# Attention and a gated MLP on one core: one up product split a second time, the softmaxes re-timed, a scheduler that looks ahead

## The chip, the cores and the metric

The kernel runs on one core of a Trainium2 chip, in one launch. The metric is the device time in microseconds, lower is better: the median of several runs, and for all reasoning one execution that was recorded by the hardware profiler.

## What is computed

The input x has 2048 rows of 1024 numbers in bf16. With xn, the layer norm of x, the result is x + s * g. s is an attention over a sliding, dilated window, projected back; g is the silu of a gated MLP on the same xn. Cut to what matters:

```
qkv = xn @ wqkv                      # 32 heads of 32
idx = pos[:, None] - 2 * arange(8)   # each row sees 8 rows: itself, 2 back, 4 back, ... 14 back
logits = einsum("bhsd,bhswd->bhsw", q, k[idx]) * 32 ** -0.5     (masked where idx < 0)
s = einsum("bhsw,bhswd->bhsd", softmax(logits), v[idx]) @ wo
h = silu(xn @ w1) * (xn @ w3)        # 3584 wide
g = silu(h @ w2)
out = x + s * g
```

## The kernel before, in words

**Blocks and chunks.** The rows are worked in two blocks of 1024 (`b` = 0, 1), each of two chunks of 512; the chunks are numbered 0 to 3. Everything is kept turned, features on the 128 partitions, tokens along the free axis. Within a block the order on TensorE is: q, k, v projections (`qkv_pairs`), in block 1 then the output projection of chunk 1 (`wo`), 14 up steps (`up_step`, each for 256 of the 3584 columns of w1 and w3), the down projection (`mlp_down`), the output projection of the block's first chunk, and at the very end that of chunk 3.

**Seven products instead of eight.** Each large product is done by a Strassen scheme: the operand pair is cut 2 x 2, and seven products of sums of the quarters take the place of eight. The two output columns blocks of an up step are gate (w1) and up (w3), the rows are the two chunks. Sums of weight quarters (`w_sums`, line 359 of the helper `tt`) are made by DVE in block 0, used there, stored to DRAM by POOL (`s_dram`) and loaded again in block 1; sums of xn quarters (`xn_sums`) lie in `xs`. In the down projection two of the products (`product2_p1`, `product2_t1`) are split a second time in the same way; their matmuls have 256 columns and line 1102, all others have line 350 (helper `mm`) and mostly 512 columns.

**An up step** has three pairs of PSUM banks, `pa`, `pe`, `pb`. On TensorE: first product into `pa` (8 matmuls), second into `pe` (8), the tail of the step before (8, into its `pb`), fourth into `pa` (8), then 8 each into `pb`, `pe` and `pb` again; the step's own tail is left for the next step. 56 matmuls in all. ACT copies the first product from `pa` into `pb` (`fork`), saves `pe` and `pb` to SBUF in between (`us5`, `us2`) and does the silus; DVE adds `ua2` (from `pe`), `uh` (from `pb`, before the tail writes there again) and multiplies `um`.

**Attention** is DVE's work. `scores(c)`: for each of 8 window positions two multiplications of 2048 elements, three additions, the last of them into `E`. `softmax(c)`: the scores are moved by 16 DMAs, alternately on POOL and SP, so that each partition has whole rows of them; DVE adds up the four parts (three additions `z` of 1024), subtracts the maximum, ACT takes the exponential (with a table load), DVE makes the sum, the reciprocal and the product, and 16 DMAs move the result back, into `E` or, for chunk 2, into a buffer of its own. `values(c)`: 16 multiplications and 14 additions of 2048 elements into `qo`. Softmax and values of a chunk lie beside the matmuls of some later stage.

**Parks.** vT and kT hold one chunk. Chunk 1's k and v, chunk 2's v and chunk 3's q, k and v are staged in h_sb, written to DRAM (`put`) and loaded when their place is free (`get`).

**What sets the order.** The kernel first lists operations with an engine, what they read and write, and an estimated duration (`Plan.op`); `place` gives buffers, `depend` finds the dependences, `limits` works back from TensorE's order to a latest start for each operation, `soon` shifts some of them. `simulate` then runs engines against each other with the estimated durations: TensorE keeps its listed order, any other engine that is free takes, of the operations that are ready, the one with the earliest limit. The resulting order is emitted and fixed: each engine works its instructions in that order, and an instruction that waits holds up everything behind it on that engine. Loads go over SP, most stores over POOL and SP, in six 1 MB buffers (`r8`).

Of the kernel before, what the change touches and what calls it, by code (L numbers as in the profile page):

```python
# [34 lines left out]
class Op:  # L35
    __slots__ = ("eng", "emit", "rd", "wr", "occ", "lat", "table", "nbytes", "pred", "succ", "n",
                 "start", "done", "ready", "limit", "name", "late", "idx", "rate", "then")


class Plan:  # L40
# [3 lines left out]
    def __init__(self):  # L44
        self.ops, self.slots, self.pools, self.wide = [], [], {}, {}
        self.shift = 0.0
        self.rate = 3e5
        self.rank, self.soon, self.chains = {}, {}, []

# [11 lines left out]
    def op(self, eng, name, emit, rd=(), wr=(), occ=0.0, lat=0.08, table=None, nbytes=0, late=0.0):  # L61
        o = Op()
        o.then = None
# [67 lines left out]
    def limits(self):  # L131
# [6 lines left out]
        for o in reversed(self.ops):  # L138
# [6 lines left out]
            o.limit = lim if o.limit is None else min(o.limit, lim)  # L145
            o.limit += o.late
# [9 lines left out]
    def simulate(self):  # L156
# [6 lines left out]
        pipe = 0.0  # L163
# [11 lines left out]
        while left:  # L175
# [13 lines left out]
            if e == PE:  # L189
                o = ops[pes[pe_at]]  # L190
                pe_at += 1
            else:
                i = min((i for i in ready[e] if ops[i].ready <= T), key=lambda i: (ops[i].limit, i))
                ready[e].remove(i)
                o = ops[i]
# [35 lines left out]
def kernel(  # L231
# [12 lines left out]
    P = 128  # L244
# [17 lines left out]
    CH_ = [r.split() for r in ("ofork0_1 exp1", "dfork1_3 exp3", "u2_l10_1 sq2", "fk_l10_1 var2_1")]  # L262
# [15 lines left out]
    s_dram = dram.tile([FB, P, 4, KH, 2 * P], FP16, name="s_dram")  # L278
    t_dram = dram.tile([P, FH, 4, CH], FP16, name="t_dram")
    park = {k: dram.tile([P, NJ, CH], BF16, name=f"park_{k[0]}{k[1]}")  # L280
            for k in (("k", 1), ("v", 1), ("v", 2), ("q", 3), ("k", 3), ("v", 3))}
# [26 lines left out]
    for n, t in plan.wide.items():  # L308
# [13 lines left out]
    nc.gpsimd.memset(maskb[:], 0.0)  # L322
    nc.gpsimd.affine_select(
        out=maskb[0:32], in_=maskb[0:32], compare_op=ALU.is_ge, fill=-1.0e9,
        base=0, pattern=[[-DIL, W], [1, HALO]], channel_multiplier=0,
    )
    nc.gpsimd.memset(kT[:, :, 0:HALO], 0.0)
# [248 lines left out]
    def halo(nm):  # L576
        b = {"k": kT, "v": vT}[nm]
        plan.op(ACT, f"halo{nm}", lambda: nc.scalar.copy(out=b[:, :, 0:HALO], in_=b[:, :, CH:CH + HALO]),
                [(nm, j) for j in range(NJ)], [(nm, j, "halo") for j in range(NJ)], 0.25, 0.11)

    def home(c, nm):

        if (nm, c) in park:
            return lambda j: (lambda: stage(c, nm, j), stage_cells(c, nm, j))
        if nm == "q":
# [4 lines left out]
    def stage_at(c, nm, j):  # L590
        if nm == "q":
            return 20 + j, 1
# [10 lines left out]
    def put(c, nm):  # L603
        cells = [x for j in range(NJ) for x in stage_cells(c, nm, j)]
        fl, _ = stage_at(c, nm, 0)
        if nm == "q":
            src = lambda: h_sb[:, fl:fl + NJ, CH:BL]
        else:
            src = lambda: h_sb[:, fl:fl + 4, :].rearrange("p f (r n) -> p (f r) n", r=2)
        dma(SP, f"put{nm}{c}", lambda: park[nm, c][:], src, cells, [("park", nm, c)], 1024)  # L610

    def get(c, nm, behind=()):
        rd = [("park", nm, c)]
        if c >= 2:
            rd.append(("step", 1, {("v", 2): 2, ("q", 3): 3, ("k", 3): 4, ("v", 3): 5}[nm, c]))
# [38 lines left out]
    def qkv_sums(wts, early=0.0, hold=([], [], [])):  # L654

        S = [plan.slot("r8", f"S{i}") for i in range(2)]
        w = lambda kh, r: (lambda: wts[kh].ap().rearrange("p (c j) -> p c j", j=NJ)[:, :, r * 4:r * 4 + 4])
# [5 lines left out]
        tt("qs2" + "f" * (early > 0), sub, sv(2), w(0, 0), w(0, 1), [wts[0]] + hold[2], c(2), 2048, True, -early)  # L663
        return S
# [71 lines left out]
    def scores(c):  # L736
# [3 lines left out]
        if ("k", c) in park:  # L740
            halo("k")
            get(c, "k", [("E", W - 1, 3, NR - 1)] if c == 1 else [("L", 2)])
        for w in range(W):
            o = HALO - DIL * w
            pr = []
            for jh in range(2):
                p_t = plan.slot("att", f"p{c}_{w}_{jh}")
                tt(f"qk{c}", mul, lambda p_t=p_t: r4(p_t), lambda jh=jh: qo[:, u, jh * 4:jh * 4 + 4, :],
                   lambda jh=jh, o=o: kT[:, jh * 4:jh * 4 + 4, o:o + CH],
                   qo_cells(u, J4[jh]) + [("k", j) for j in J4[jh]] + ([("k", j, "halo") for j in J4[jh]] if w else []),  # L750
# [8 lines left out]
               [p0], [("E", w, sq, r) for sq in range(4) for r in range(NR)], 512, True)  # L759

    def softmax(c):

        zf = lambda a: (lambda: a().bitcast(FP32))
        if c != 2:
            sl = [plan.slot("att", f"sm{c}_{i}") for i in range(3)]
# [856 lines left out]
```

## Time and profile before

| | us |
|---|---|
| median of 3 runs (lowest, highest) | 712.68 (712.26, 712.99) |
| the profiled execution | 712.41 |
| its span, first to last instruction | 710.6 |
| stretch from 30 to 130 us: DVE busy | 99.9 of 100 |
| up steps of block 1, 340 to 600 us: DVE busy | 247.0 of 260 |
| granted TensorE clock | 1.00 throughout |

The profiled execution's time is its span and 1.8 us around it. "Busy" is the time in which an engine had an instruction running. In the timeline a row has its start, its length, the engine, the line of the kernel (often that of a helper), the output and inputs by their buffers' names, the shape, and the number of instructions merged in it; behind it, in brackets, the idle time before it and what ended that. A matmul's row lasts longer than its share of the stream, since matmuls overlap; the distance between starts is what counts.

### The profile page before, as it was taken

How to read it: one execution, taken by the hardware profiler on the slowest of the kernel's cores; microseconds unless marked ns; L12 is line 12 of the kernel's file. 1: busy time of each engine (PE TensorE's matmuls, PEld its weight loads, DVE VectorE, ACT ScalarE, POOL GpSimd, SP SyncE). 2: the span in 40 equal slices, each digit the busy share in tenths (PEclk: the TensorE clock that was granted, in tenths of full speed). 3: DMA queues.
4: the chain of work that ended last, by engine and by line, in shares of the span. 5: the costliest groups of instructions: out<-in, count | busy, mean ns of one | idle time of the engine just before them, and what ended most of it. 6: DMA issues, size and time to landing. Idle time of an engine off the chain costs nothing.

```text
span 710.6 us, 9461 instructions
## 1 busy us (share of the span) xinstructions
PE 704.8 (99%) x3510; PEld 359.2 (51%) x3510; DVE 670.4 (94%) x806; ACT 385.8 (54%) x674; POOL 47.0 (7%) x96
## 2 busy tenths in 40 slices
PE   8999999999999999999999999999999999999998
PEld 5555544444444474744555554444444445656443
DVE  8999999797999999997899999968999997999996
ACT  7644556575656799422535355658565655422233
POOL 1010100202000000002200000020200011020000
PEclk9999999999999999999999999999999999999999
DMA  9999976659545757793654559786653557648503
GB/s 333 289 367 321 322 277 208 207 203 265 200 144 192 257 185 185 178 302 122 221 173 145 178 199 314 260 267 192 174 192 119 183 180 231 208 137 293 178 1 118
DMA packets 131197, 151.35 MB, mean 213 GB/s; under 512 B 17104, under 2 KB 109136, under 8 KB 125904
## 3 DMA queue, kind: packets, MB, share of 16 engines
q1 hardware_dynamic: 121392, 123.03, 54.7%
q0 software_dynamic: 5104, 26.22, 10.0%
q10 hardware_dynamic: 4656, 1.51, 1.0%
q8 instruction: 27, 0.44, 0.3%
q14 instruction: 18, 0.15, 0.1%
HBM read 106.96 MB, written 32.51 MB: 196 GB/s over the span
## 4 chain that ended last, share of the span: by engine, by line
PE 96%; ACT 2%; DVE 1%; DMA 1%; issue 0%; SPq 0%; DVEq 0%; ACTq 0%
PE mm L350 90%; PE mm L1102 6%; ACT r L474 1%; ACT k L364 1%; DMA r<-in_A_x_dram 1%; ACT k L479 0%; PE mm L529 0%; DVE small L447 0%; ACT L806 0%; DVE r L463 0%; DVE xT L359 0%; ACT a L806 0%; ACT h_sb L381 0%; PE mm L375 0%; SPq L387 0%
## 5 line engine op out<-in xcount | busy, mean ns | idle before, releaser
L350 PEld LDWEIGHTS <-r 128*128 128x128 f16 (+1 forms) x2276 | 240.2, 107 | 244.0 <-DMA r<-in_A_wqkv_dram 0.4
L350 PE MATMUL mm<-xs,r 128*128 128x512 f16 x1280 | 295.3, 379 | 0.0
L350 PE MATMUL mm<-xT,r 128*128 128x512 bf16 (+1 forms) x996 | 227.2, 372 | 0.1
L364 ACT COPY k<-mm 128x512 f32<-128x512 f32 (+1 forms) x200 | 115.1, 579 | 75.3 <-PE mm L350 68.4
L350 PE MATMUL mm<-r,h_sb 128*128 128x512 f16 (+1 forms) x592 | 129.6, 379 | 0.0
L350 PEld LDWEIGHTS <-h_sb 128*128 128x128 f16 (+1 forms) x688 | 67.3, 98 | 80.3 <-issue 0.6
L364 ACT COPY mm<-mm 128x512 f32<-128x512 f32 (+1 forms) x105 | 56.4, 541 | 59.6 <-PE mm L350 41.0
L359 DVE TENSOR_TENSOR a<-a,a 128x2048 bf16<-128x2048 bf16 (+1 forms) x68 | 82.6, 1215 | 0.1
L359 DVE TENSOR_TENSOR a<-qo,kT 128x2048 bf16<-128x2048 bf16 x64 | 77.0, 1215 | 0.1
L381 ACT ACTIVATE k<-k 128x512 bf16<-128x512 f32 x56 | 33.0, 625 | 68.3 <-DVE k L359 68.2
L359 DVE TENSOR_TENSOR r<-r,r 128x1024 f16<-128x1024 bf16 (+6 forms) x71 | 60.0, 851 | 0.7 <-DMA xT<-r 0.5
L359 DVE TENSOR_TENSOR h_sb<-mm,k 128x512 bf16<-128x512 f32 (+1 forms) x68 | 59.2, 900 | 0.7 <-PE mm L350 0.7
L359 DVE TENSOR_TENSOR h_sb<-h_sb 128x1024 f16<-128x1024 bf16 (+7 forms) x55 | 43.9, 822 | 7.1 <-DMA h_sb<-E 3.6
L359 DVE TENSOR_TENSOR a<-E,vT 128x2048 bf16<-128x2048 bf16 x42 | 49.7, 1215 | 0.0
L359 DVE TENSOR_TENSOR k<-mm,k 128x1024 f32<-128x1024 f32 (+1 forms) x44 | 44.8, 1022 | 3.7 <-PE mm L350 3.7
L381 ACT ACTIVATE h_sb<-mm 128x512 bf16<-128x512 f32 x60 | 35.8, 599 | 17.6 <-PE mm L350 16.9
L364 ACT CAST k<-mm 128x512 bf16<-128x512 f32 x56 | 32.6, 587 | 13.5 <-PE mm L350 13.5
L359 DVE TENSOR_TENSOR h_sb<-h_sb,k 128x2048 bf16<-128x2048 bf16 x28 | 34.1, 1217 | 6.1 <-ACT k L364 6.1
L359 DVE TENSOR_TENSOR qo<-qo,a 128x2048 bf16<-128x2048 bf16 x32 | 38.9, 1214 | 0.0
L359 DVE TENSOR_TENSOR a<-a 128x1024 bf16<-128x1024 bf16 (+4 forms) x53 | 33.7, 638 | 2.4 <-ACT a L806 2.2
L359 DVE TENSOR_TENSOR r<-r 128x1024 f16<-128x1024 bf16 (+3 forms) x37 | 28.7, 801 | 0.0
L387 POOL DMA_DIRECT2D a<-E x24 | 12.5, 527 | 174.1 <-DVE E L359 95.3
(120 smaller groups left out, 480.6 us busy)
## 6 DMA issues: line engine op xcount, KB each, us to landing
r<-in_B_w_dram SPq DMA_DIRECT2D x42, 512.0 KB, 5.0
s_dram<-r POOLq DMA_DIRECT2D x14, 1024.0 KB, 5.4
r<-t_dram SPq DMA_DIRECT2D x16, 896.0 KB, 7.1
r<-s_dram SPq DMA_DIRECT2D x14, 1024.0 KB, 5.0
r<-in_B_w_dram SPq DMA_DIRECT2D x12, 896.0 KB, 5.5
r<-in_A_wqkv_dram SPq DMA_DIRECT2D x10, 1024.0 KB, 7.2
h_sb<-in_B_w_dram SPq DMA_DIRECT2D x14, 512.0 KB, 9.1
t_dram<-h_sb POOLq DMA_DIRECT2D x7, 1024.0 KB, 5.5
```

The source lines that it names most:

```text
L350: nc.tensor.matmul(cut(ps.ap()), lhsT=lhs[k](), rhs=cut(rhs[k]()), start=(first and k == 0), stop=(last and k == n - 1), skip_group_check= ...
L359: plan.op(DVE, name, lambda: fn(out=o(), in0=a(), in1=b()), rd, wr, occ, 0.08, late=late)
L364: plan.op(ACT, name, lambda: nc.scalar.copy(out=o(), in_=a()), rd, wr, occ, 0.11)
L381: plan.op(ACT, name, lambda: nc.scalar.activation(out=o(), in_=a(), func=ACTF.Silu), rd, wr, occ, 0.11, table="silu")
L387: plan.op(eng, name, lambda: e.dma_start(out=o(), in_=a()), rd, wr, occ, 0.0, nbytes=kb * 1024, late=late)
L474: plan.op(ACT, f"mean{c}_{st}", lambda i=i, st=st: nc.scalar.activation(out=xrow(xt, st), in_=xrow(xt, st), func=ACTF.Copy, scale=1.0 / D, ...
L1102: nc.tensor.matmul(half(bank.ap, n)(), lhsT=a[k](), rhs=c[k](), start=first and k == 0, stop=k == NQ - 1, skip_group_check=True)
```

## The change

1. **A second split in the up stage.** In block 1, from step 1 on, the first product (into `pa`) is made of seven products of half-size matmuls, two each, in four parts that are put between the products of the step before (`up_first`). It needs sums of w1's quarters (`w_sums2`, made by DVE in block 0 for steps 1 to 13, stored by POOL, loaded on SP with 256 KB a step) and of the first chunk's xn (`x_sums2`, four sums, once). Between the parts stand three ACT copies of 256 columns and one DVE addition (`ucc`) of 512.
2. **Moves in halves.** As soon as four of the eight window positions are there, their scores are moved (`gather`), in four DMAs of twice the size in place of eight; the additions `z` and the product behind the reciprocal are made in halves as well, and each half of the result is moved back by itself.
3. **Places.** Softmax 2 and 3 work in h_sb (rows of it that late up steps fill). k3 isn't parked but written to h_sb, where the scores read it; v2 stays staged in h_sb and is copied to vT by one DMA.
4. **Softmax 3** is listed behind the scores of chunk 3, in the up stage ahead of values 2; before it stood behind the output projection of chunk 2.
5. **The scheduler** simulates three times ahead of the real one and notes when each operation became ready. An ACT or DVE operation is now held back, and the engine left idle, if it would run past the time at which a more urgent one is to become ready and would make that one late.
6. The masks for the first rows are made in a scratch buffer and spread by a small DMA at the start.

```diff
+            o.need = o.limit
             o.limit += o.late
...
+                for i in sorted((i for i in ready[e] if ops[i].ready <= T), key=lambda i: (ops[i].limit, i)):
+                    o = ops[i]
+                    end = T + o.occ + (1.29 if o.table and o.table != table else 0.0)
...
+                            if q.start is None and q is not o and q.limit < o.limit:
+                                hurt = end - max(q.need + lag, q.eta)
+                                if hurt > 0.05 + self.look[e] * (q.eta - T):
+                                    hit = q
+                                    break
...
+        for _ in range(self.passes):
+            self.simulate()
+            for o in self.ops:
+                o.eta = o.ready
...
-            for k in (("k", 1), ("v", 1), ("v", 2), ("q", 3), ("k", 3), ("v", 3))}
+            for k in (("k", 1), ("v", 1), ("q", 3), ("v", 3))}
...
-            get(c, "k", [("E", W - 1, 3, NR - 1)] if c == 1 else [("L", 2)])
+            get(c, "k", [("E", W - 1, 3, NR - 1)])
+        if c == 3:
+            halo("k", c)
...
+            if w % 4 == 3:
+                gather(c, w // 4)
...
+    def gather(c, i):
+        sm_places(c, i)
+        L, Lc = SM[c][i][0:2]
+        for r in range(NR):
+            dma((POOL, SP)[r % 2], f"L{c}", lambda r=r: L()[:, r * 512:(r + 1) * 512],
+                lambda r=r: E[r:P:NR, :, 4 * i:4 * i + 4].rearrange("p q w n -> p q (w n)"),
...
-        tt(f"z{c}", add, zv, lambda: Lv(0)[:, 0], lambda: Lv(0)[:, 1], LC[0] + LC[1], zc, 1024, False)
...
+        for i in range(2):
...
+            tt(f"z{c}", add, zi, part(0), part(1), Lc[i](0) + Lc[i](1), zc[i], 512, False)
+            tt(f"z{c}", add, zi, zi, part(2), Lc[i](2) + zc[i], zc[i], 512, False)
+            tt(f"z{c}", add, zi, zi, part(3), Lc[i](3) + zc[i], zc[i], 512, False)
...
+            if b in U2B and fb:
+                dma(SP, f"s2.{fb}", lambda: s2_v(wt).rearrange("p q k n -> p (q k n)"),
+                    lambda: s2_dram[fb].rearrange("p q k n -> p (q k n)"), [("sd2", fb)], [(wt, 1, 0)], 256)
...
+        tt("wss0", add, S(0), A(1, 0), A(1, 1), Ac, Sc(0), 256, True)
+        tt("wss2", sub, S(2), A(0, 0), A(1, 0), Ac, Sc(2), 256, True)
+        tt("wss1", sub, S(1), S(0), A(0, 0), Ac + Sc(0), Sc(1), 256, True)
+        tt("wss3", sub, S(3), A(0, 1), S(1), Ac + Sc(1), Sc(3), 256, True)
...
+    def up_first(b, fb):
...
+            plan.op(PE, "mu " + pa[i].name, emit, A[1] + B[1], [pa[i]], 2 * 0.1097, 0.0)
+
+        p(1, 0, a(0, 0), x(0, 0), True)
+        p(1, 1, s_(0), t(0))
+        s5 = plan.slot("k2", "us5p")
+        cp(f"ufork{b}_{fb}", half(pa[0].ap, 0), half(pa[1].ap, 0), [pa[1]], [pa[0]], 0.27)
+        cp("us5p", half(lambda: f32(s5), 0), half(pa[1].ap, 1), [pa[1]], [s5], 0.27)
+        yield
+        p(1, 0, s_(1), t(1))
+        p(0, 0, a(0, 1), x(1, 0))
+        cp(f"usnap{b}_{fb}", half(pa[0].ap, 1), half(pa[1].ap, 0), [pa[1]], [pa[0]], 0.27)
+        yield
+        p(1, 0, s_(2), t(2))
+        p(0, 1, s_(3), x(1, 1))
...
+        both = lambda: pa[0].both().rearrange("p b n -> p (b n)")
+        tt(f"ucc{b}", add, lambda: both().rearrange("p (b h n) -> p b h n", b=2, h=2)[:, :, 1],
+           lambda: both()[:, HC:3 * HC].rearrange("p (b n) -> p b n", b=2),
+           lambda: f32(s5)[:, 0:HC].unsqueeze(1).to_broadcast([P, 2, HC]), [pa[0], pa[1], s5], [pa[0], pa[1]], 512, False)
+        yield
+        p(1, 0, a(1, 1), t(3))
...
     def up_step(b, fb):
-        for i in I:
+        for i in I if not two else ():
             mm(pa[i], wl(0, 0, i), bx[0, 0], True, [(wt, 0, 0)] + xt_cells(0, 0), mark=[("step", b, fb)])
...
             mm(pb[i], sl(1, i), tx[1], False, [(st, 1)] + xs_cells(1))
...
+        next(more, None)
             mm(pe[i], sl(3, i), bx[1, 1], False, [(st, 3)] + xt_cells(1, 1))
...
+        next(more, None)
             mm(pb[i], sl(2, i), tx[2], False, [(st, 2)] + xs_cells(2))
+        next(more, None)
...
                 mm(pb[i], wl(1, 1, i), tx[3], False, [(wt, 1, 1)] + xs_cells(3))
+                if i == 0:
+                    next(more, None)
...
             if b and fb == 5:
                 softmax(c0)
                 scores(c1)
+                softmax(c1)
...
-    softmax(3)
     values(3)
```

More of the change, by code (lines that the diff above doesn't have):

```diff
@@ L36 @@
     __slots__ = ("eng", "emit", "rd", "wr", "occ", "lat", "table", "nbytes", "pred", "succ", "n",
-                 "start", "done", "ready", "limit", "name", "late", "idx", "rate", "then")
+                 "start", "done", "ready", "limit", "name", "late", "idx", "rate", "then", "need", "eta")
 class Plan:
@@ L48, in __init__ @@
         self.rank, self.soon, self.chains = {}, {}, []
+        self.look, self.passes = {ACT: 0.0, DVE: 0.0}, 3
     def slot(self, pool, name):
```

248 lines of the change are left out of this document (178 added, 70 removed).

## The prediction, made before the changed kernel was run

> **What bounds the kernel now.** I read the page first: the busy shares and the chain of work that ended last.
>
> ```profile
> PE 704.8 (99%) x3510; PEld 359.2 (51%) x3510; DVE 670.4 (94%) x806; ACT 385.8 (54%) x674; POOL 47.0 (7%) x96
> PE 96%; ACT 2%; DVE 1%; DMA 1%; issue 0%; SPq 0%; DVEq 0%; ACTq 0%
> ```
>
> TensorE is busy 99% of the span and makes 96% of the chain. Matmuls overlap, so busy time alone doesn't say that the stream is dense; the chain in order of time does.
>
> ```profile
> 341.84 257.45 PE mm L350 x1192
> ...
> 604.08 7.67 PE mm L1102 x70
> ```
>
> 1192 full matmuls (512 columns) in 257.45 us are 0.216 us each; 70 half-size ones (256 columns, line 1102) in 7.67 us are 0.1096 each. With 0.216 and 0.1096 I went along TensorE's timeline and looked for starts later than the count before them explains. From 20 us to the end only two are over 0.1 us.
>
> ```profile
> 253.58 1.89 PE L350 MATMUL mm<-xs,r 128*128 128x512 f16 x8
> 255.53 0.93 PE L1102 MATMUL mm<-r,h_sb 128*128 128x256 bf16 x7
> ...
> 337.95 3.62 PE L350 MATMUL mm<-h_sb 128*128 128x512 f16 x16
> 341.84 1.89 PE L350 MATMUL mm<-h_sb 128*128 128x512 f16 x8 [0.27 <-ACT k L364]
> ```
>
> 253.58 + 8 x 0.216 = 255.31, and the next starts at 255.53: 0.22 us. 337.95 + 16 x 0.216 = 341.41 against 341.84: 0.43 us. So TensorE issues without holes, and only two things change the time: fewer columns, or new holes. A hole comes where DVE is late, so DVE comes next, by stretches (columns: PE, PEld, DVE, ACT, POOL busy, clock, DMA).
>
> ```profile
> 130.00:180.00 50.00, 50.00 (x234) 22.65 (x232) 40.50 (x49) 32.35 (x55) 10.58 (x20) 1.00 0.74 234
> 320.00:340.00 20.00, 20.00 (x94) 9.11 (x93) 14.45 (x18) 7.65 (x12) 3.47 (x7) 1.00 0.45 147
> 340.00:460.00 120.00, 119.73 (x556) 63.87 (x554) 119.90 (x144) 60.90 (x107) 4.23 (x8) 1.00 0.63 211
> 460.00:490.00 30.00, 30.00 (x141) 13.56 (x139) 21.24 (x24) 19.68 (x33) 4.17 (x8) 1.00 0.72 228
> 490.00:584.00 94.00, 94.00 (x437) 42.57 (x436) 94.00 (x95) 55.39 (x97) 4.24 (x8) 1.00 0.53 169
> 584.00:600.00 16.00, 16.00 (x79) 7.64 (x78) 11.88 (x11) 7.99 (x15) 4.17 (x8) 1.00 0.81 248
> 600.00:690.00 90.00, 90.00 (x512) 49.82 (x510) 89.97 (x102) 27.91 (x50) 4.23 (x8) 1.00 0.54 171
> sum 710.00, PE 704.75 PEld 359.16 DVE 670.45 ACT 385.77 POOL 47.04; mean PE 64.07 PEld 32.65 DVE 60.95 ACT 35.07 POOL 4.28
> ```
>
> The reader is to see that DVE is a second bound behind the first: full over long stretches, idle mainly in four, 9.5, 5.6, 8.8 and 4.1 us (28 of its 39.6; most of the rest is start and end).
>
> **The change, part by part. TensorE's columns.** In block 1, steps 1 to 13, the first up product (8 full matmuls) becomes seven products of two half-size ones. Removed 8 x 0.216 = 1.728 us, added 14 x 0.1096 = 1.534; per step -0.194, in 13 steps **-2.5 us**. Nothing covers TensorE, so all of it counts. That half-size matmuls hold their pitch between full ones is seen at 250.5 to 253.6 us, where 28 of them stand between full groups.
>
> ```profile
> 250.52 1.69 PE L1102 MATMUL mm<-r,h_sb 128*128 128x256 bf16 x14
> 252.05 1.69 PE L1102 MATMUL mm<-xT,xs 128*128 128x256 f16 x14
> ```
>
> 28 in 3.06 us (to 253.58) are again 0.109 each. The Trainium skill speaks against this: "TensorE: Matmul & The Clock Gate", Back-to-back issue gap, gives for a stream of weight loads and matmuls about 131 ns at 512 columns and 81 ns at 128, an estimate of some 98 ns at 256. By that page the edit would cost 13 x (14 x 98 - 8 x 131) ns, 4.2 us more instead of 2.5 less; the trace, with 216 and 109.6 ns, doesn't agree, and decides.
>
> **DVE's new work.** Pitches come from repeated rows, since an instruction's row overlaps the next by about 0.08 us.
>
> ```profile
> 359.48 3.49 DVE L359 TENSOR_TENSOR a<-E,vT 128x2048 bf16<-128x2048 bf16 x3
> 416.35 2.47 DVE L359 TENSOR_TENSOR h_sb<-mm,k 128x512 bf16<-128x512 f32 x4
> 464.17 0.75 DVE L359 TENSOR_TENSOR E<-a 128x512 bf16<-128x512 bf16 x2
> 707.51 0.48 DVE L359 TENSOR_TENSOR xT<-xT 128x256 bf16<-128x256 bf16 x2
> ```
>
> So 2048 two-byte elements take (3.49 - 1.21)/2 = 1.14 us, 512 from PSUM (2.47 - 0.68)/3 = 0.60, 512 two-byte ones 0.34, 256 of them 0.20. Added in block 0: 13 steps x 4 weight sums x 0.20 = 10.4. In block 1: 13 adds `ucc` x 0.60 = 7.8, and four sums of the moving operand 4 x 0.34 = 1.4. Each softmax has four instructions more on the same elements, 4 x 0.07; four of them 1.1. Together **+20.7 us**: 670.4 becomes 691 of about 708. Hidden only if DVE's idle stretches fill.
>
> **What fills them.** The four idle stretches are the softmaxes. For two of them:
>
> ```profile
> 469.52 1.22 DVE L359 TENSOR_TENSOR h_sb<-h_sb 128x1024 f32<-128x1024 bf16 x1 [1.94 <-DMA h_sb<-E]
> 475.09 2.48 DVE L359 TENSOR_TENSOR h_sb<-h_sb 128x1024 f32<-128x1024 f32 x2 [1.71 <-DMA h_sb<-E]
> 485.75 0.69 DVE L359 TENSOR_TENSOR h_sb<-h_sb 128x512 f32<-128x512 f32 x1 [3.27 <-ACT h_sb L806]
> 590.70 1.09 DVE L359 TENSOR_TENSOR xs<-h_sb 128x1792 f16<-128x1792 bf16 x1 [2.23 <-PE mm L350]
> ```
>
> Around 470 to 486 DVE waits for the moved scores, then for the exponential, and has no other work: the scores of chunk 3 need k3, whose load is issued behind the moves and takes this long to land (last column, median us):
>
> ```profile
> kT<-park_k SPq DMA_DIRECT2D x2, 1024.0 KB, 11.5
> vT<-park_v SPq DMA_DIRECT2D x3, 1024.0 KB, 7.4
> L806 ACT ACT_TABLE_LOAD x4 | 5.1, 1283 | 0.1
> ```
>
> After the change k3 lies in h_sb, so these scores can run from 466 us on; moves in halves let half of the sums start earlier. Softmax 3 (about 9 us of DVE) goes ahead of values 2 into the up stage, so values 2 reaches into 584 to 600. What moves with it: its 16 DMAs, and on ACT an exponential with a table load before it and one behind it (1.28 each), over 2.6 us in one step of 11.9; on an engine 54% busy I cost it at nothing, and at up to 1 us if a bank's copy stands behind it. A cover is lost too: v3's load (7.4 us) starts when values 2 ends and used to lie under softmax 3; now the sums of the down projection, due then anyway, lie over it. Of the 28 us I take 20 as filled: 9 of the 15.1 in block 0, where the 256-element sums are free to wait, and 11 of the 12.9 in block 1.
>
> **The wait that the split adds.** Parts of the next step's product now stand between products, each behind a copy on ACT or an add on DVE, and the 8 matmuls that opened a step are gone. That shortens one old deadline, `uh`:
>
> ```profile
> 454.07 1.89 PE L350 MATMUL mm<-xT,r 128*128 128x512 bf16 x8
> 455.80 3.62 PE L350 MATMUL mm<-xs,r 128*128 128x512 f16 x16
> ...
> 454.69 1.22 DVE L359 TENSOR_TENSOR h_sb<-mm,k 128x1024 bf16<-128x1024 f32 x1
> ...
> 466.36 1.23 DVE L359 TENSOR_TENSOR h_sb<-mm,k 128x1024 bf16<-128x1024 f32 x1 [0.30 <-PE mm L350]
> ```
>
> The sums that `uh` reads end about 454.07, `uh` ends at 455.91, and TensorE wants its bank back after two groups of 8, 3.46 us after 454.07. Afterwards only four half-size matmuls and one group lie between: 0.44 + 1.73 = 2.17 us. An idle DVE needs 0.2 + 1.23 = 1.43 (the second row starts 0.20 after the sums end at 466.16). So 0.74 us are left. A score instruction just begun on DVE (1.14) makes it 2.57: a hole of 0.40. Behind `uh` stands `ucc`, done at 1.43 + 0.68 = 2.11; the last pair, which writes the half that `ucc` reads, starts at 2.17 + 0.86 = 3.03, so 0.9 is left, and the two copies that start the next step's banks have about as much. If the phase between the engines is left to chance, the mean hole is 0.40 x 0.40/(2 x 1.14) = 0.07 per step, 0.9 us in 13; the ends are 0 and 13 x 0.40 = 5.2. The new rule of the scheduler leaves DVE and ACT idle ahead of an urgent instruction, so I take 0.6. The same rule could take the two old holes: 0 to 0.65 us, I take 0.3, since the first stands behind one long ACT instruction, which ended only at 255.1:
>
> ```profile
> 253.95 1.17 ACT L479 ACTIVATE k<-r,small 128x1024 bf16<-128x1024 bf16 x1
> ```
>
> **Queues.** ACT gets three 256-column copies a step, 0.37 each by the row below, 1.1 of 11.9 us: nothing. The moves are 8 instead of 16 per direction of a softmax, so POOL and SP issue less. Each step loads 256 KB more on SP, and the weights are wanted some 5 us earlier.
>
> ```profile
> 527.19 5.16 SPq L387 DMA_DIRECT2D r<-in_B_w_dram x2
> r<-in_B_w_dram SPq DMA_DIRECT2D x42, 512.0 KB, 5.0
> L364 ACT COPY mm<-mm 128x256 f32<-128x256 f32 x17 | 6.3, 371 | 10.9 <-PE mm L1102 9.3 <-PE mm L350 1.2
> ```
>
> The second of the pair, the weights of the step after next, is issued near 532 and lands near 537; its first use was the step at 550.8, and is now about 5 us before: 8 us remain, so nothing. Startup and output stay.
>
> **The sum**, against the profiled execution's 712.41 (span 710.6; the median of the runs is 712.68, 0.27 above): 712.41 - 2.5 - 0.3 + 0.6 = **710.2 us**, 0.35% below the median.
>
> **Rivals.** (1) *The gain is eaten.* If in most steps `uh`, `ucc` and the copies come 0.15 to 0.25 us late, 13 x 0.2 = 2.6 us and the time is 712.4. For it: DVE is full, and 0.74 us is less than one instruction. Against: before, with as full a DVE, no hole stands in any up step.
>
> (2) *DVE becomes the bound, and the kernel is slower.* The place is the last output projection.
>
> ```profile
> 690.86 0.68 DVE L359 TENSOR_TENSOR h_sb<-qo,h_sb 128x1024 f16<-128x1024 bf16 x1
> ...
> 693.51 5.34 PE L350 MATMUL mm<-h_sb 128*128 128x512 f16 x24
> ```
>
> DVE ends the sums of the third values' output at 691.5; the products over them start at 693.5, the last sum is wanted near 697, some 5.5 us later. TensorE will be 2.8 earlier, so 2.7 remain. From 340 us on block 1 adds 7.8 + 1.4 + 0.5 = 9.7, and block 0 may hand on 10.4 + 0.6 less the 9 that fill there, 2. If of the 12.9 idle in 460 to 490 and 584 to 600 less than 9.7 + 2 - 2.7 = 9.0 fills, TensorE waits at the end: that is the deciding point (I took 11). With 4 filled it is 5 late, 710.2 + 5 = 715.2; with none, 719.2. For it: 691 of 708 leaves little room, and the rule that leaves DVE idle costs room as well. Against: the largest waits lose their cause (k3).
>
> (3) *Half-size matmuls in pairs don't hold 0.1096.* If each showed its own weight load,
>
> ```profile
> L350 PEld LDWEIGHTS <-r 128*128 128x128 f16 (+1 forms) x2276 | 240.2, 107 | 244.0 <-DMA r<-in_A_wqkv_dram 0.4
> ```
>
> 0.107 more, a step would grow by 14 x 0.107 and the kernel by 19.5 us: 729.7. The 70 in 7.67 us, and the 28 between full groups, speak against it; a step alone differs, since it has pairs in place of sevens. The section of the Trainium skill named above ("TensorE: Matmul & The Clock Gate", Back-to-back issue gap) would give, by its own figures, 712.4 + 4.2 = 716.6 for the same edit.
>
> **Chances.** Forecast 0.58 (709.2 to 711.2), rival 1 0.22 (711.3 to 714.1), rival 2 0.18 (714.1 to 719.2), rival 3 0.02. A measurement tells about 0.2% (1.43 us) from no change: faster below 711.25, slower above 714.1, so 0.58, 0.22, 0.20. The low end is all of 2.5 and both old holes, 709.2; the high end takes in rival 1 and the likelier half of rival 2: 709.2 to 715.5.
>
> **What would show it.** TensorE: 104 full matmuls fewer, 182 half-size more, no gap over 0.1 us in the up steps of block 1 (else rival 1). DVE: about 691 busy, little idle at 460 to 490. The wait of TensorE for DVE after 680 us shows rival 2. The forecast is wrong if the old holes stay and the new ones pass 1.5 us together.

## The result, and the profile after

The changed kernel takes 711.39 us in the median (711.06 to 711.86, 18 runs), the kernel before 712.70 beside it (712.26 to 713.96, 18 runs). The ratio is 0.9981, with a 95% interval of 0.9975 to 0.9987: 1.3 us or 0.19% faster; the interval leaves out 1, and the value is just short of the 0.2% that the prediction took as its bound. 710.2 was forecast, so the kernel is 1.2 us slower than that. The profiled execution took 711.14 us, with a span of 709.4.

The page of the changed kernel, to be held against the two lines of before:

```profile
PE 703.0 (99%) x3588; PEld 366.9 (52%) x3588; DVE 690.1 (97%) x891; ACT 391.6 (55%) x713; POOL 38.6 (5%) x79
...
PE 96%; DVE 2%; ACT 1%; issue 0%; DVEq 0%
...
L1026 PE MATMUL mm<-xT,r 128*128 128x256 f16 (+1 forms) x182 | 28.4, 273 | 0.0
```

TensorE's chain has nearly the same shares; DVE went from 670.4 to 690.1 us. The last row is the split itself, 182 half-size matmuls, 14 in each of 13 steps. (Its mean of 273 ns is the length of a row; the distance of starts, below, is what counts.)

DVE by stretches (columns: PE, PEld, DVE, ACT, POOL busy, clock, DMA), the four in which it idled before:

```profile
130.00:180.00 50.00, 50.00 (x234) 22.67 (x232) 47.52 (x76) 32.56 (x55) 8.15 (x15) 1.00 0.74 241
320.00:340.00 20.00, 20.00 (x95) 9.08 (x93) 18.32 (x27) 7.52 (x12) 1.07 (x2) 1.00 0.43 139
460.00:490.00 30.00, 30.00 (x158) 15.36 (x157) 30.00 (x36) 18.99 (x39) 1.07 (x2) 1.00 0.55 189
584.00:600.00 16.00, 16.00 (x92) 8.90 (x91) 15.97 (x16) 6.90 (x14) 0.00 (x0) 1.00 0.24 76
```

Its idle time there was 9.5, 5.6, 8.8 and 4.1 us, and is 2.5, 1.7, 0 and 0. From 340 to 690 us, where block 1 is worked on, DVE is now idle for 1.0 us in all. (The up steps of block 1 run from about 430 to 597 us in this execution; what lies between 340 and 430 are the projections.)

TensorE's timeline around a step's seams and at the first product behind the up stage:

```profile
428.86 1.89 PE L390 MATMUL mm<-r,h_sb 128*128 128x512 bf16 x8
...
439.22 0.60 PE L1026 MATMUL mm<-xT,r 128*128 128x256 bf16 x4
439.66 1.89 PE L390 MATMUL mm<-xT,r 128*128 128x512 bf16 x8
...
597.40 1.69 PE L1272 MATMUL mm<-r,h_sb 128*128 128x256 bf16 x14
```

A group of four half-size matmuls lasts 439.66 - 439.22 = 0.44 us, 0.11 each, as forecast, and between full ones. The two other rows serve below.

The holes of the changed kernel, on TensorE and on the engine that it waits for (a hole is the time by which a group of matmuls starts later than the count of matmuls before it explains):

```profile
253.78 1.89 PE L390 MATMUL mm<-xs,r 128*128 128x512 f16 x8
...
254.78 1.15 ACT L519 ACTIVATE k<-r,small 128x1024 bf16<-128x1024 bf16 x1
...
255.91 0.38 ACT L404 COPY mm<-mm 128x256 f32<-128x256 f32 x1
...
256.34 0.92 PE L1272 MATMUL mm<-r,h_sb 128*128 128x256 bf16 x7 [0.68 <-ACT mm L404]
...
284.31 1.23 DVE L399 TENSOR_TENSOR a<-qo,kT 128x2048 bf16<-128x2048 bf16 x1
...
286.45 0.63 DVE L399 TENSOR_TENSOR r<-xs 128x896 f16<-128x896 f16 x1
...
287.14 1.05 PE L1272 MATMUL mm<-r 128*128 128x256 f16 x8 [0.23 <-DVE r L399]
```

The eight matmuls from 253.78 end their share at 255.51, the next starts at 256.34: 0.83 us, where the kernel before had 0.22. The 256-column copy that it needs stands behind layer-norm instructions of 1.15 us on ACT. At 287.14 there is a second one, 0.40 us (0.09 before): the sum of DVE that it waits for began only at 286.45, behind the score multiplication of 284.31 and one more sum. The only one in an up step of block 1 is at 503.17, 0.18 us; its copy stands on ACT behind a silu and the table load that follows the exponential of softmax 2:

```profile
500.95 1.28 ACT L421 ACT_TABLE_LOAD   x1
...
502.25 0.60 ACT L421 ACTIVATE h_sb<-mm 128x512 bf16<-128x512 f32 x1
...
502.74 0.38 ACT L404 COPY mm<-mm 128x256 f32<-128x256 f32 x1
...
503.17 0.60 PE L1026 MATMUL mm<-xT,r 128*128 128x256 f16 x4
```

The old hole of 0.43 us at 341.84 is gone.

**The account** goes by the last group of matmuls, which started at 706.02 us before and starts at 704.44 now, 1.58 us earlier: columns -2.53, hole at 342 us -0.43, hole at 256 us +0.61, at 287 us +0.31, one up step (at 503 us) +0.18, down projection (at 610 us) +0.12, and +0.2 from the first 20 us, where the loads of the start decide. From that group to the end of the span it was 4.58 us and is 4.96; in the executions of the twelve experiments it is 4.7 to 5.5, with nothing changed there, so I take these 0.4 us as the scatter of single executions; that is not shown further.

### The profile page after: what moved, and what is told of

The parts are those of the page before. It is cut to its first block, busy times and chain, and to the rows that moved or that the text cites. A ratio compares the mean times of both kernels' runs of the same rounds, so it can differ in the third digit from the quotient of the medians.

```text
span 709.4 us, 9725 instructions
## 1 busy us (share of the span) xinstructions
PE 703.0 (99%) x3588; PEld 366.9 (52%) x3588; DVE 690.1 (97%) x891; ACT 391.6 (55%) x713; POOL 38.6 (5%) x79
## 4 chain that ended last, share of the span: by engine, by line
PE 96%; DVE 2%; ACT 1%; issue 0%; DVEq 0%
PE mm L390 87%; PE mm L1272 5%; PE mm L1026 3%; PE mm L372 1%; DVE a L399 1%; ACT k L519 0%; DVE h_sb L399 0%; ACT r L514 0%; PE mm L569 0%; DVE r L399 0%; DVE xT L399 0%; ACT k L404 0%; ACT xT L576 0%; DVE r L503 0%; ACT h_sb L421 0%
## 5 line engine op out<-in xcount | busy, mean ns | idle before, releaser
L390 PEld LDWEIGHTS <-r 128*128 128x128 f16 (+1 forms) x2172 | 229.8, 107 | 221.0 <-DMA r<-in_A_wqkv_dram 0.8
L390 PE MATMUL mm<-xT,r 128*128 128x512 bf16 (+2 forms) x892 | 202.6, 371 | 0.2 <-ACT small L492 0.2
L404 ACT COPY k<-mm 128x512 f32<-128x512 f32 (+1 forms) x213 | 119.6, 567 | 79.5 <-PE mm L390 72.5
L404 ACT COPY mm<-mm 128x512 f32<-128x512 f32 (+1 forms) x131 | 66.4, 510 | 84.3 <-PE mm L390 40.1
L399 DVE TENSOR_TENSOR a<-a,a 128x2048 bf16<-128x2048 bf16 (+3 forms) x70 | 79.6, 1138 | 0.2
L399 DVE TENSOR_TENSOR a<-qo,kT 128x2048 bf16<-128x2048 bf16 x48 | 58.6, 1229 | 0.1
L399 DVE TENSOR_TENSOR h_sb<-h_sb 128x1024 f16<-128x1024 bf16 (+7 forms) x74 | 53.8, 759 | 0.0
L399 DVE TENSOR_TENSOR r<-r 128x256 f16<-128x256 bf16 (+3 forms) x89 | 44.0, 509 | 0.0
L399 DVE TENSOR_TENSOR a<-a 128x1024 bf16<-128x1024 bf16 (+4 forms) x48 | 30.6, 638 | 2.3 <-ACT a L888 2.1
L1026 PE MATMUL mm<-xT,r 128*128 128x256 f16 (+1 forms) x182 | 28.4, 273 | 0.0
```

Of the source, the lines that this page charges most:

```text
L390: nc.tensor.matmul(cut(ps.ap()), lhsT=lhs[k](), rhs=cut(rhs[k]()), start=(first and k == 0), stop=(last and k == n - 1), skip_group_check= ...
L399: plan.op(DVE, name, lambda: fn(out=o(), in0=a(), in1=b()), rd, wr, occ, 0.08, late=late)
L404: plan.op(ACT, name, lambda: nc.scalar.copy(out=o(), in_=a()), rd, wr, occ, 0.11)
L1026: nc.tensor.matmul(half(pa[i].ap, n)(), lhsT=A[0][k](), rhs=B[0][k](), start=first and k == 0, stop=k == 1, skip_group_check=True)
```

## The experiments

All twelve were timed beside the kernel before; ratios are to that, with their intervals. The first two take the change apart.

**1. Everything but the split.**

```diff
-    U2B = (1,)
+    U2B = ()
```

> The changed kernel with the second split taken out (the first up product is again 8 full matmuls in every step; no sums of weight quarters, no ucc, no 256 KB loads); scheduler, softmaxes, moves and places as changed. Theory A (the gain is the columns: 13 x 0.194 = 2.5 us, and the rest of the edit moves holes about): 2.5 us come back and the one hole of 0.18 us in an up step of block 1 goes, 711.4 + 2.5 - 0.2 = 713.7 us, between 713.0 and 714.1, so slower than the kernel before by 0.5 to 1.3; DVE busy falls from 690 to about 670 us. Rival B (the split pays for itself at most, and scheduler and softmaxes bring the 1.3 us): 711.0 to 711.8 us.

Measured: 713.15 us, ratio 1.0004 (0.9996 to 1.0013). Theory A, near its lower end: without the split the rest of the change is worth nothing. The split's own worth is read between two points that both timelines have, here without the split:

```profile
428.64 1.89 PE L390 MATMUL mm<-r,h_sb 128*128 128x512 bf16 x8
...
599.58 0.60 PE L1272 MATMUL mm<-r,h_sb 128*128 128x256 bf16 x4
```

170.94 us here and 597.40 - 428.86 = 168.54 with the split: 2.40, and 2.58 without the hole at 503 us, against 2.53 by columns. The hole at 256 us is 1.26 us here, so it doesn't need the split. That at 287 us isn't there; it isn't there with the split either when the moves are whole (the eleventh experiment), so it belongs to the order that the scheduler finds.

**2. The split alone**, all of point 1 of the change, put into the kernel before:

```diff
 (the kernel before)
+    U2B = (1,)
...
+        two = b in U2B and fb > 0
+        more = up_first(b, fb + 1) if b in U2B and fb + 1 < FB else iter(())
...
+        if b in U2B:
+            x_sums2()
```

> The kernel before with the second split alone: its matmuls, weight sums, loads, copies and ucc, and nothing of the scheduler, the softmaxes, the moves and the places of k3 and v2. Theory A (DVE is the second bound, and its new work is hidden only because the softmaxes' idle stretches were opened by the other edits): DVE gets 13 x 4 x 0.20 + 13 x 0.60 + 4 x 0.34 = 19.6 us more, of which little finds room; TensorE then waits for DVE at the stage ends, in the last output projection above all: 719 us if some 9 us are late, up to 730 if nearly all is, and DVE still idles some 20 us or more in the softmaxes. Rival B (the split hides by itself): 712.7 - 2.5 + 0 to 0.6, so 710.2 to 710.8 us.

Measured: 738.75 us, ratio 1.0364 (1.0350 to 1.0378): theory A, and worse than its upper end. What TensorE waited for, in total, times, longest:

```profile
PE mm L1190 <- DVE r L361: 6.2, 2, 3.4
PE mm L352 <- DVE r L361: 5.7, 4, 3.5
PE mm L352 <- DVE h_sb L361: 5.5, 1, 5.5
```

17 us of waiting for DVE, in the down projection and the last output projections. A further part of the 26 us is in the clock column behind the stalls:

```profile
611.00:614.00 3.00, 2.83 (x14) 2.04 (x15) 2.46 (x4) 0.00 (x0) 0.00 (x0) 0.50 1.01 340
614.00:617.00 3.00, 3.00 (x16) 2.14 (x15) 1.90 (x3) 0.91 (x2) 0.00 (x0) 0.50 1.05 350
617.00:620.00 3.00, 3.00 (x23) 2.11 (x22) 2.73 (x4) 2.37 (x5) 0.88 (x2) 1.00 0.95 320
701.00:703.00 2.00, 1.62 (x4) 0.58 (x5) 2.00 (x3) 0.00 (x0) 0.00 (x0) 0.50 0.00 0
```

After a stall of 3.5 us that ended at 611.2 the granted clock is 0.50 for 6 us, and 26 matmuls take twice their pitch, 2.8 us more; after one of 5.7 us that ended at 701.4 and one of 3.7 that ended at 715.7 it is so again.

**3. No look-ahead.**

```diff
-        self.look, self.passes = {ACT: 0.0, DVE: 0.0}, 3
+        self.look, self.passes = {ACT: 0.0, DVE: 0.0}, 0
```

> The changed kernel with the scheduler's look-ahead off (no simulations ahead, so nothing is ever held back); all else as changed. Theory A (the look-ahead keeps holes out of the up steps): the hole of 0.43 us near 342 comes back, that near 256 falls from 0.84 to between 0.2 and 0.5, and the up steps of block 1 get holes of 0.07 to 0.2 us a step in the mean, 0.9 to 2.6 in 13: together 712.0 to 713.8 us. Rival B (the up steps have slack enough, and the look-ahead only moved the old holes): 711.0 to 711.6 us, and no hole over 0.2 us in the up steps of block 1.

Measured: 711.93 us, ratio 0.9990 (0.9981 to 0.9999). Between the two. The hole at 342 us is back (0.43), that at 256 us is 0.31, that at 287 us is 0.67, and two up steps of block 1 have holes, 0.18 and 0.43. The larger of them:

```profile
515.17 0.60 PE L1026 MATMUL mm<-xT,r 128*128 128x256 f16 x4
515.35 1.22 DVE L399 TENSOR_TENSOR a<-qo,h_sb 128x2048 bf16<-128x2048 bf16 x1
...
516.49 1.22 DVE L399 TENSOR_TENSOR h_sb<-mm,k 128x1024 bf16<-128x1024 f32 x1
...
517.76 1.02 PE L390 MATMUL mm<-xs,r 128*128 128x512 f16 x4 [0.26 <-DVE h_sb L399]
```

`uh` (the addition of 1024 from PSUM, at 516.49) waits behind a score multiplication begun at 515.35, when its sums had just ended (the half-size group behind them starts at 515.17), and TensorE waits for `uh`: the mechanism that the prediction priced at 0.40 us a time. It struck twice in 13 steps, 0.6 us, and with the look-ahead not once. But in the changed kernel's order the look-ahead also goes with most of the hole at 256 us: it holds layer-norm instructions back on ACT for copies (one that runs at 245.78 without it runs at 247.95 with it), and they are all the later ahead of the copy that TensorE waits for. That this follows from the rule itself is not shown: with the look-ahead on and whole moves (the eleventh experiment) the hole is 0.32. On balance the look-ahead is worth about 0.6 us by the medians; the two intervals overlap a little.

**4. Softmax 3 back behind the output projection of chunk 2.**

```diff
                 softmax(c0)
                 scores(c1)
-                softmax(c1)
...
+    softmax(3)
     values(3)
```

> The changed kernel with softmax 3 put back to where it stood before, behind the output projection of chunk 2 and ahead of values 3, its buffers in the attention pool as before; split, scheduler, k3 in h_sb and moves in halves as changed. Theory A (the fill of DVE's idle stretch at softmax 3 is needed): with nothing beside it DVE waits for the moves and the exponential again, 4 to 9 us, while DVE ends the sums for the last output projection only 5.9 us ahead of TensorE's use (686.0 against 691.9 us); the end slips, 712.5 to 717 us, and TensorE waits for DVE after 680 us. Rival B (its place doesn't matter, since DVE is ahead by 5.9 us at the end): 711.2 to 711.8 us.

With the place go the buffers of softmax 3, which are those of before, and the moves of its scores, which are issued when all eight window positions are there.

Measured: 717.86 us, ratio 1.0073 (1.0059 to 1.0087): theory A, 0.9 us above its upper end.

```profile
692.59 1.22 DVE L399 TENSOR_TENSOR h_sb<-r,h_sb 128x2048 f16<-128x2048 bf16 x1
693.73 0.68 DVE L399 TENSOR_TENSOR r<-mm,k 128x512 bf16<-128x512 f32 x1
...
694.46 3.60 PE L390 MATMUL mm<-h_sb,qo 128*128 128x512 f16 x8 [3.53 <-DVE r L399]
...
697.85 1.49 PE L390 MATMUL mm<-h_sb 128*128 128x512 f16 x3
```

TensorE waits 3.53 us for an addition of DVE that stands behind values 3 and a weight sum; the eight matmuls from 694.46 then take 3.39 us in place of 1.73. The windows show the clock:

```profile
694.00:697.00 3.00, 2.54 (x7) 0.81 (x7) 3.00 (x5) 0.61 (x2) 0.00 (x0) 0.50 0.00 0
697.00:700.00 3.00, 3.00 (x9) 1.08 (x8) 3.00 (x6) 1.86 (x4) 0.00 (x0) 0.50 0.00 0
```

**5. The copies near 256 us put first on ACT.**

```diff
-... "u2_l10_1 sq2", "fk_l10_1 var2_1")]
+... "u2_l10_1 sq2", "fk_l10_0 var2_3", "fk_l10_1 var2_0")]
```

> The changed kernel with one listing rule more on ACT: the first 256-column copy near 256 us goes ahead of the second of the three long layer-norm instructions (1.15 us each) that it stands behind, the second copy ahead of the third. Theory A (the hole of 0.84 us there is only that queue): the copy starts 1.1 to 2.3 us earlier, the hole falls to 0.1 to 0.4, and nothing else changes: 710.6 to 711.0 us. Rival B (DVE is so full that a shift at 256 us moves its whole later order, and the changed kernel has a deadline that the kernel before had not: softmax 3 works in rows of h_sb that the up steps from 541 us on write, and its instructions stand between 1.2 us ones of values 2): if softmax 3 ends some us later, TensorE waits near 565 us for the silu that writes those rows, 2 to 4 us, and behind a stall of 3.5 us or more its pitch is doubled for some 3 to 6 us, as in the split alone: 712.5 to 717 us.

Measured: 715.67 us, ratio 1.0039 (1.0027 to 1.0052). The hole fell from 0.83 to two of 0.37 and 0.17, and rival B came true 300 us later:

```profile
560.21 1.06 ACT L888 ACTIVATE h_sb<-h_sb 128x1024 f32<-128x1024 f32 x1
...
562.18 0.68 DVE L399 TENSOR_TENSOR h_sb<-h_sb 128x512 f32<-128x512 f32 x1
...
562.85 1.09 ACT L421 ACTIVATE h_sb<-mm 128x512 bf16<-128x512 f32 x2
...
563.50 2.75 PE L390 MATMUL mm<-xs,r 128*128 128x512 f16 x12 [1.04 <-ACT h_sb L421]
...
577.26 1.22 DVE L399 TENSOR_TENSOR a<-r,vT 128x2048 bf16<-128x2048 bf16 x1
...
578.39 1.22 DVE L399 TENSOR_TENSOR h_sb<-mm,k 128x1024 bf16<-128x1024 f32 x1
...
579.67 1.02 PE L390 MATMUL mm<-xs,r 128*128 128x512 f16 x4 [2.40 <-DVE h_sb L399]
```

The exponential of softmax 3 ends at 561.3, the first addition of its sum (562.18) claims the rows of h_sb in which the scores arrived, the silu of an up step that writes those rows begins at 562.85, and TensorE starts 1.20 us late. The claim alone doesn't set the time of the silu: the table load that follows the exponential on ACT ends at 562.83, within 0.03 us of that addition. DVE's later order no longer fits: `uh` stands behind a multiplication of values 2 (577.26) and TensorE loses another 2.56 us, and then the clock:

```profile
580.00:582.00 2.00, 2.00 (x9) 0.85 (x7) 2.00 (x3) 1.74 (x4) 0.00 (x0) 0.68 0.00 0
582.00:584.00 2.00, 2.00 (x6) 0.76 (x5) 2.00 (x3) 0.92 (x2) 0.00 (x0) 0.50 0.49 92
```

**6, 7 and 8. Copies first, with the rows set free and more simulations.** The additions of softmax 2 and 3 don't touch the rows that they claim; the claim is needed only where the buffer is shared.

```diff
-... zmc + LC[0], 512, False)
+... zmc + (LC[0] if c < 2 else []), 512, False)
...
-... cell + (LC[1] + pbc if not i else []), 512, False)
+... cell + ((LC[1] if c < 2 else []) + pbc if not i else []), 512, False)
...
-        self.look, self.passes = {ACT: 0.0, DVE: 0.0}, 3
+        self.look, self.passes = {ACT: 0.0, DVE: 0.0}, 5
```

> The run with the copies ahead, and two more edits: the maximum and the product of softmax 2 and 3 no longer claim the rows of the moved scores (they don't touch them there), so that these rows come free after the sums z; and five simulations ahead in place of three. Theory A (the rows' claim is what makes a late softmax 3 stop TensorE): no hole near 565 us whatever the order on DVE, the hole at 256 us 0.1 to 0.5 and that at 287 us under 0.5: 710.3 to 711.0 us, below the changed kernel. Rival B (the softmax is late for its own sake, and other stages are as near their deadlines): a stall of 1 us or more moves elsewhere, to the steps near 457 us or to the down projection near 610 us: 711.5 to 714 us.

Then each of the two edits by itself:

> The run with the copies ahead and the rows of the moved scores freed early, but three simulations ahead as in the changed kernel: the rows alone. Theory A (the claim on the rows is what stopped TensorE near 565 us): no stall there; what DVE is late by shows at the next deadline, in the down projection near 612 us, 1 to 1.5 us: 711.3 to 712.8 us. Rival B (the five simulations made the difference): the stalls of 1.2 and 2.6 us and the doubled pitch stay, 714.5 to 716 us.

> The run with the copies ahead, the rows claimed as in the changed kernel, and five simulations ahead: the simulations alone. Theory A (the rows' claim decides): TensorE still stalls near 563 us, 1 to 2.5 us in all, with little or no doubled pitch: 711.8 to 714 us. Rival B (the order of five simulations is right without more): 710.3 to 711.0 us, as with both edits.

Measured: both 710.65 us, ratio 0.9968 (0.9956 to 0.9980); the rows alone 711.92, 0.9989 (0.9979 to 0.9998); the simulations alone 711.65, 0.9989 (0.9980 to 0.9999). Theory A in all three for the place: with the rows free TensorE doesn't stall near 563 us, with five simulations alone it does, by 1.20 us (its time is 0.15 us below the range of theory A). With the rows alone 0.27 us are lost at 612 and 0.63 at 642, so the lateness did move on, as B had it for the first. Both edits together leave 0.36 and 0.17 us at 256 to 258, 0.43 at 299 and 0.18 in an up step.

How the claim stops TensorE is seen at the silu that writes the rows, on ACT. The first row is the changed kernel, the other two the run with five simulations alone:

```profile
561.38 0.60 ACT L421 ACTIVATE h_sb<-mm 128x512 bf16<-128x512 f32 x1
...
561.36 1.28 ACT L421 ACT_TABLE_LOAD   x1
...
562.65 1.09 ACT L421 ACTIVATE h_sb<-mm 128x512 bf16<-128x512 f32 x2
```

With the rows free this silu runs at 555.33 us (both edits) and 555.74 (the rows alone), ahead of the exponential of softmax 3. With the claim it has to wait for an addition behind the exponential, and so stands behind the table load as well. In the run with five simulations that addition ends at 561.80, and it is the table load, to 562.64, that holds the silu up. The changed kernel has the same delay; it only meets it with about 1 us to spare (its first silu ends at 561.98, and the group of matmuls that was late in the other runs starts at 563.05).

**9. More work for DVE.** Four multiplications of the scores of chunk 2 are made twice, with the same result.

```diff
+                if c == 2 and jh == 0 and w < 4:
+                    tt(f"qk{c}", mul, lambda p_t=p_t: r4(p_t), ...
```

> The changed kernel with four multiplications of the scores of chunk 2 made twice: 4 x 1.14 = 4.6 us more for DVE, early in the up stage of block 1, and nothing else. Theory A (DVE has to be ready only at the end, and is 5.9 us ahead there, 686.0 against 691.9 us): all of it is hidden, 711.2 to 711.8 us. Rival B (DVE is the second bound at every deadline on the way: h_sb's rows for the late up steps, the sums of the down projection): TensorE waits for most of the 4.6 us somewhere between 500 and 640 us, and longer by its doubled pitch if the wait is 3.5 us or more at one place: 714 to 719 us.

Measured: 715.11 us, ratio 1.0036 (1.0024 to 1.0049), by the ratios 0.55% or 3.9 us above the changed kernel, for 4.6 us of DVE work: rival B, at its low end.

```profile
PE mm L390 <- DVE h_sb L399: 2.4, 1, 2.4
...
PE mm L390 <- ACT h_sb L421: 1.0, 1, 1.0
```

These are the same two stalls as in the fifth experiment, 1.20 us at 564.4 and 2.55 at 580.6. At the end, in the changed kernel, DVE is far ahead:

```profile
685.35 0.72 DVE L399 TENSOR_TENSOR h_sb<-qo,h_sb 128x1024 f16<-128x1024 bf16 x1
...
691.92 1.24 PE L390 MATMUL mm<-h_sb 128*128 128x512 f16 x5
```

Its sums for the last output projection end at 686.1 and are used at 691.9. That lead of 5.8 us hides nothing, since other deadlines come first.

**10. k3 parked again.**

```diff
-    ... for k in (("k", 1), ("v", 1), ("q", 3), ("v", 3))}
+    ... for k in (("k", 1), ("v", 1), ("q", 3), ("k", 3), ("v", 3))}
```

> The changed kernel with k3 parked as before: written to DRAM and loaded into kT when the scores of chunk 2 are done; all else as changed. Theory A (the prediction's step: the scores of chunk 3 filled DVE's idle stretch from 460 to 490 us because k3 lay ready in h_sb): DVE idles there again for the 11.5 us of the load less what else is ready, 5 to 9 us; as 4.6 us more of DVE work cost 3.7 us, nearly all of that comes back as waits of TensorE near 565 us and in the down projection, longer where the pitch doubles: 716 to 722 us. Rival B (the moves in halves and softmax 3 in the up stage give DVE enough else to do): 711.2 to 713 us.

Measured: 720.33 us, ratio 1.0107 (1.0093 to 1.0121): theory A.

```profile
473.41 0.59 SPq L427 DMA_DIRECT2D kT<-park_k  x1
...
477.21 1.23 DVE L399 TENSOR_TENSOR k<-mm,k 128x1024 f32<-128x1024 f32 x1 [3.28 <-PE mm L390]
```

The load of k3 is issued at 473.41, and DVE idles 3.28 us ahead of 477.21 and 5.0 in 460 to 490 us. TensorE then waits 3.9 us for a silu near 567 us, where the rows of softmax 3 are due, and goes on at the halved clock for 7 matmuls; in the down projection it loses another 2.5 us, in holes of 0.81, 1.35 and 0.38.

**11. Whole moves.**

```diff
-            if w % 4 == 3:
-                gather(c, w // 4)
+            if w == W - 1:
+                gather(c, 0)
+                gather(c, 1)
```

> The changed kernel with the scores moved only when all eight window positions are there (the DMAs as large as changed, all eight issued at the end); the additions stay in halves. Theory A (the prediction's step: the moves in halves let half of the sums start earlier and so fill the softmaxes): DVE waits 2 to 4 us more in each of four softmaxes, some of it in block 1, where nothing is spare: 712.5 to 716 us. Rival B (with k3 in h_sb and softmax 3 beside values 2 DVE has other work while scores travel, so that the halves bring nothing): 710.5 to 711.6 us.

Measured: 710.51 us, ratio 0.9975 (0.9967 to 0.9984), against 0.9981 for the changed kernel (the intervals overlap): rival B. That the scores move in halves fills nothing (the additions and the moves back are still in halves here):

```profile
460.00:490.00 30.00, 29.84 (x156) 15.30 (x158) 30.00 (x35) 18.17 (x38) 1.07 (x2) 1.00 0.53 176
```

DVE is as full as with halves, and so it is from 584 to 600 us; in the two stretches of block 0 it is idle for 4.4 us, against 4.2. The holes differ (0.32 at 256, 0.46 at 342, 0.18, 0.23, none at 287), which is the order's doing.

**12. Whole moves, and softmax 3 due 5 us earlier.**

```diff
+    plan.soon.update({n + "3": -5.0 for n in ("z", "tr", "zd", "exp", "rec", "pb")})
```

> The run with whole moves, and softmax 3's instructions on DVE and ACT listed as due 5 us earlier (those of values 2 beside it run later for it). Theory A (what is left over in the up steps and after them is the lateness of softmax 3 and what stands behind it): no hole over 0.2 us from 340 us on, only one of 0.2 to 0.4 us near 256: 710.0 to 710.7 us, 1.0 to 1.4 below the changed kernel or level with the run with the rows free. Rival B (the shift only moves the lateness to values 2 and the down projection near 610 us): 711.0 to 713 us.

Measured: 710.08 us, ratio 0.9963 (0.9950 to 0.9977), the fastest of all, with an interval that just touches the changed kernel's and overlaps those of the sixth and the eleventh experiment: theory A. From 20 us on two holes are left, 0.32 us at 256 and 0.18 in an up step, and its last group of matmuls starts at 703.09, 2.93 us before that of the kernel before. The columns were worth 2.53 and the holes of before 0.65 more: the gain that the split allows is there, in an order that loses little elsewhere.

## Why the prediction was right, and where it was off

**Columns, right.** 104 full matmuls fewer and 182 half-size more, 0.11 us each between full ones: 2.58 us against 2.53. The page that spoke against it ("TensorE: Matmul & The Clock Gate" of the Trainium skill, Back-to-back issue gap) doesn't fit the timeline of the changed kernel either.

**The old holes, the step that failed.** I took 0.3 us off for them. One went (0.43), but the other, which the prediction itself put down to one long ACT instruction, grew by 0.61, and one that I had passed over as small, at 287 us, by 0.31. Together +0.5 in place of -0.3: most of the 1.2 us. The term rested on the rule that keeps urgent instructions free, which looks only at what is protected: what is held back comes later, and whatever stands behind it waits longer. For the hole at 256 us this is a likely reading and no more: it was 0.83 us in the changed kernel, and 1.26, 0.31, 0.32 and 0.32 in the first, third, eleventh and twelfth experiment, whose ACT has the same work there. For the hole at 287 us it doesn't hold, since that is 0.67 without the look-ahead. What the runs show is that the two follow the order that the simulation happens to find.

**New holes in the up steps, right in kind and too large.** 0.6 us was forecast for 13 steps, and 0.18 is there, in one step. It is on ACT, behind the table load that I had costed at nothing and at up to 1 us; without the look-ahead `uh` loses 0.6 where the estimate from chance gave 0.9. Rival 1 is not what happened, though the time falls in its band (711.3 to 714.1 us, chance 0.22) and the gap of 0.18 is over the 0.1 us that was named as its sign: it asked for a loss in most steps, and twelve of the 13 have none. With a gain of 1.3 us for a forecast 2.5 the range was met because it was wide enough to take rival 1 in.

**DVE's work and its cover, right in size.** 691 us were forecast and 690.1 are busy; of the 28 idle us I took 9 and 11 as filled, and 10.9 and 12.9 were. Of the reasons, k3 (9 us slower without it) and the place of softmax 3 with its buffers (6.5 us) are shown to carry it; the moves of the scores in halves, named beside them, are shown not to.

**Rival 2 was the danger, and too cheap.** Its place was given as the last output projection, with 2.7 us of room. That is where it strikes when softmax 3 is late, but 4.6 us of work cost 3.9 at an earlier place, which the prediction had not seen: the rows of h_sb in which softmax 3 works are written by up steps from about 560 us on. I had told of the place in h_sb as a cover gained (k3 at hand) and not as a deadline added. That the changed kernel meets this deadline is, as far as the prediction goes, luck: with two copies exchanged 300 us earlier it doesn't, and 715.67 us would have been outside the range. And the price was counted as the wait alone, 715.2 to 719.2 us; without the cover it is 738.8, with 17 us of waits and a halved clock behind the long ones.

**What stays open.** Why the order of the changed kernel meets the deadline near 563 us, and the one with two copies exchanged 300 us earlier doesn't, is only followed back one step: the exponential of softmax 3 starts at 557.47 us in the one and at 560.21 in the other. Why it is 2.7 us later there is not shown; DVE's order is found by simulation, and with DVE full a small shift moved deadlines 300 us on.

## What to carry to other kernels

A saving on the bound engine that is paid for on a second, nearly full one is worth what the second engine's idle stretches can take: here 2.5 us in the up stage with the cover (1.3 for the kernel), and a loss of 26 without, so the cover is the change, and the saving its small fruit. Ask of every buffer that is moved into shared space who writes there next; it is a deadline, and a claim that is wider than the use brings it forward. When the order is made by a planner, the effect of a local mend is read at every later deadline, not at the place of the mend.

## What the runs showed of the hardware

A stall of TensorE costs more than its length. After stalls of 3.5 to 5.7 us the granted clock was 0.50 and the pitch (the distance of starts) doubled for 3 to 6 us, some 1.5 to 2.8 us more; stalls of 1.5 us and less never did it. Between, it went both ways: 2.56 us that ended at 579.7 did (the fifth experiment), 2.55 that ended at 580.6 (the ninth) and 2.96 that ended at 655.5 (the second) didn't.

The record of the clock in these traces tells more. The halved stretches last 3.41 us (580.74 to 584.15 in the fifth experiment) or twice that (610.18 to 617.01 in the second), and within an execution all changes lie whole multiples of 3.413 us apart: 81.92 us, or 24 times that, from 617.01 to the next fall at 698.93. So there is a grid that runs on whatever the stalls do. In the cell before the fall at 580.74 TensorE was idle for 2.34 of the 3.41 us. The stall that ended at 580.6 lies across a border of its grid (578.60), with 0.58 us in one cell and 1.97 in the next; that which ended at 655.5 lies across 654.56, with 2.07 and 0.89. In these runs 2.07 us of idle time in a cell left the clock alone and 2.34 halved it, and where a stall lies on the grid is chance.

The Trainium skill ("TensorE: Matmul & The Clock Gate", Part 1: The HAM clock gate) says that activity is watched in a free-running window of some 3.4 us, and that the clock is halved after an idle window and full again after a busy one. The grid and its length agree with it; that 2.34 us of idle time in a cell were enough says that the window need not be wholly idle.
